# Q split low half first, two copies of each attention unit issued as DMAs, and partition changes in the planner's costs

## The chip, the cores and the metric

One NeuronCore of a Trainium2 chip runs the whole program. The metric is device time in microseconds of one execution. Engines are named as in the profile: PE (TensorE), DVE (VectorE), ACT (ScalarE), POOL (GpSimd) and SP (SyncE, which issues every DMA of this kernel).

## The reference

Attention with a learned decay bias, then two feed-forward stages, each on the output of the one before. Shapes: q, k, v are (4, 8, 576, 64), x is 2304 tokens by 512, and the hidden sizes are 2048 and 1536.

```
scores = q @ k.T / sqrt(D)                      # per batch and head, causal
cum    = cumsum(max(s, 0));  bias = min(-(cum_i - cum_j), 0)
attn   = softmax(where(causal, -1e9, scores + bias));  o = attn @ v
x  = o laid out as (B*S, H*D)
h  = x @ w_in;  x = (h - tanh(h)) @ w_out       # first stage
a  = x @ w_a;  b = x @ w_b;  out = (a * b) @ w_out2   # second stage
```

## The kernel before

Every fp32 matrix is split into two fp16 halves, a high one and a low one, and a product is made of three fp16 products: high with high, high with low, low with high. The work is cut into blocks of 256 tokens. A block j of attention has four units, one for each pair of heads; there are eight blocks and 32 units. Blocks 0 to 3 hold the first two tiles of 128 queries of a batch, blocks 4 to 7 the last two and the 64 rows that are left over (a "merged" unit, with pool "rest" and longer keys). The first feed-forward stage of a block runs as soon as its attention is done and shares the engines with the attention of later blocks. The second one comes last.

The path of one unit, with the names that the text uses. `g_load` issues the loads of q, k and v, `g_scale` works out powers of two for scaling, `u_split` writes the halves of q and k into the tile qk, and writes three rows of ones, scaled, into qB at partitions 64 to 66. `u_turn` transposes qk with one DMA into qkT: the first 64 partitions of qkT are then the first halves that were stored, the last 64 the second ones. The score product is made of two matmuls (`u_qk`): one of qkT with qkT over 128 partitions, one of qB with kB over 67 partitions, of which the last three carry the bias (kB rows 64 to 66 come by a small DMA, `u_load`).

The high half of q is stored first, so that qkT holds q high in partitions 0 to 63 and q low in 64 to 127, beside k high and k low in the same places. `u_turn` (lines 1079 to 1081) then makes three copies of 64 partitions: k high into kB, q low into qB, and q high over q low in qkT (the doubled half). With these, the 128-row matmul gives q high with k high and with k low, and the 67-row one gives q low with k high and the bias. Each copy may run on ACT, DVE or POOL (`copy_scaled`, an `either` of three engines).

What sets the order. The program records each operation in a `Plan`, and `run` then simulates five queues (PE, DVE, ACT, POOL, SP): at each moment it takes from the ready operations of a free engine the one with the earliest due time, chooses the engine of an `either` by the costs in `cost`, and emits it. The due times are written out, one for each operation, in the string ORDER (four characters each), which `follow` reads only if their number is that of the recorded operations. On the chip each engine runs its instructions in the emitted order and waits for semaphores. Tiles come from pools with fixed numbers of buffers (qkT 3 and kB 3 in blocks 0 to 3, 2 each in the merged ones; qB 2; qk 2, and 1 in the merged ones). POOL operations that read, and some of DVE, take turns at a port that they share (`shares`, `lock`). All DMAs, transposes too, go through SP's one queue in emitted order.

Since all operations are emitted by one wrapper, most of the profile's rows carry line 648; tiles tell them apart.

Of the kernel before, what the change touches and what calls it, by code (L numbers as in the profile page):

```python
# [14 lines left out]
F32 = mybir.dt.float32  # L15
# [23 lines left out]
    "IbhkIAOqH/9fIACMIADLH/8mIAVxIAX4IAavIAZiIAIWIAZ7IAazIAmEIARbIAYGIAMIIAm2IAjXIAcWIAYQIATCIASAH/1qH/9TIAI2IAJoIAAmIAAZH//a"  # L39
    "H/+fIAUcIAXaIAWaIAXHIAXcIAZiIATlIAWBIATOIAWXIAXXIAQIIAYgIAU3IAQbIAHjIAYLIAVzIAUcIAVoIAWNIAX3IAdiIAeEIAdUIAgYIAQ/IAhOIAfd"  # L40
    "IAU8IAhJIAirIAjVIAizIAj3IAmPIAgTIAnDIA06IAPGIAfaIAftIAQ5IAg/IAhcIAjpIAj5IAkMIAp8IAk0IAojIA0iIAr3IA/sIAc+IAj+IAfdIAg0IAd2"
    "IAh0IAYLIAnGIAnzIAseIAhCIAtqIAyXIAnAIAxXIAwZIA1uIA3EIA1rIA6lIBE5IA7xIA6aIAdYIAy3IA2CIAxgIA2zIAuvIA2eIA6zIA68IA9rIA66IA+6"
    "IA9HIBCAIBJYIAaxIAUpIAdBIAXnIAZuIAXpIAeSIAe3IAd1H//qIAb1IAhDIAekIAmCIAfnIAgsIAj7IAk8IAmfIAh5IAizIBC/IAhXIAjmIAmhIAlmIAnv"
    "IAqiIAqKIAqtIAziIA0RIA6+IA71IA70IA/fIA/OIA/pIBAvIA3jIBEkIBD8IBASIBAUIBDFIA6MIA+wIA/SIA7XIA4uIA8pIBFdIBDaIBCEIBDEIBBNIBDG"
    "IBHlIBQJIBSaIAfNIAluIAuMIAq6IAtjIA81IAmuIA9eIA8HIA/sIBCRIBAyIBGAIBChIBGtIBHoIBPeIBICIBOPIBVBIBMSIBWrIBIXIBCmIBKHIBLwIBGz"
    "IBL9IBLBIBLQIBIwIBQvIBL6IBToIBSxIBQTIBV6IBcrIEStIENAICz+IC52ICoQIClqICtCIClFICUkICNxICQwIAmXIAx6IA2hIA6BIAh8IAheIAm9IAz+"
    "IA3gIBERIBGfIBP4IBXFIBi6IBmPIBpMIBI3IBWNIBaxIBb2IBfcIBsRIBxbIB0YIBfIIBqTIBwPIBw/IBrtIB1TIB4+IB6DICAAIB9IICE7ICGLICAZICFq"
    "ICJRICMxICSNICX7ICcmICg6IBxlICD4ICQAICmiICSnIChnICitICpiICtxIC5PIDCGIDC5ICz1IDCYIDEGIDKuIDKrIDlZIDT0IDZVIBV8IBe6IBYDIBjL"
    "IBhrIBhPIBfmIBtVIBgjIBnVIBUjIBooIBZ0IBlyIBnTIBo2IBwpIBthIB06IBzlIB0fIB1IIB40IB7XIB8IIB+nICBcICC7ICFvICIQIB+SICKlIB/RICFL"
    "ICCZIBx+ICT5ICV2ICn7ICaUICOKIB9dICOXICShICHHICStICdKICa8ICT7ICflIChzICh4ICoBICW9ICu6IC3MIC2/IC3NIC+XIC7BICqxICwvICxfICvf"  # L50
# [175 lines left out]

# [114 lines left out]
class Plan:  # L341
# [140 lines left out]
    def run(self, switch=None):  # L482
# [1348 lines left out]
```

## Time and profile before

| | |
|---|---|
| time, median of 3 runs | 974.56 us (972.02 to 976.58) |
| profiled execution | 972.53 us |
| its span, first to last instruction | 970.8 us |
| PE busy | 907.7 us (94%), 7974 matmuls |
| DVE, ACT, POOL busy | 794.6, 557.3, 211.0 us |
| granted TensorE clock, mean | 0.995 |
| DMA | 109.23 MB, mean 113 GB/s |

The share of an engine is an average over stages that differ. The attention with the first feed-forward stage takes the span up to some 575 us, the second feed-forward stage the rest. A row of the window view gives the busy time of each engine in one stretch, and what is missing to the length of the stretch is idle time.

### The profile page before, as it was taken

To read this page: it belongs to the slowest core of one execution; us is meant where nothing else is said; L and a number is where in the kernel's file an instruction comes from. 1 tells how busy PE (TensorE), PEld (TensorE's weight loads), DVE (VectorE), ACT (ScalarE), POOL (GpSimd) and SP (SyncE) were. 2 spreads that over 40 slices of the span, in tenths; PEclk is the share of its full clock that TensorE was granted. 3 is DMA by queue.
4 is the path that set the end of the run, shared out by engine and by line. 5 is a ranking of instruction groups with operands and counts; after the bars stand their busy time and mean duration, and the time that the engine had idled before them with its cause. 6 is when DMAs were issued, how large, how long until landed. Compare 5 with 4: busy or idle time off the path is not lost.

```text
span 970.8 us, 21004 instructions
## 1 busy us (share of the span) xinstructions
PE 907.7 (94%) x7974; PEld 686.0 (71%) x7974; DVE 794.6 (82%) x2038; ACT 557.3 (57%) x1112; POOL 211.0 (22%) x322
## 2 busy tenths in 40 slices
PE   1699899999999989999999999999999999999998
PEld 0477678877777777777888877544477777777865
DVE  8899999789999899898899899997277478545635
ACT  6899889767887688786898653331131232112311
POOL 2132222213443454452112200110021011000000
PEclk9999999999999999999999999999999999999999
DMA  8999764348997687989755410200020011001001
GB/s 205 224 313 278 162 131 105 73 115 168 188 189 161 133 168 155 180 184 159 264 210 182 149 45 12 76 1 1 1 88 1 1 45 44 1 1 44 1 1 44
DMA packets 255973, 109.23 MB, mean 113 GB/s; under 512 B 216897, under 2 KB 239665, under 8 KB 255873
## 3 DMA queue, kind: packets, MB, share of 16 engines
q1 hardware_dynamic: 255872, 107.90, 46.6%
q8 instruction: 62, 1.02, 0.4%
q14 instruction: 39, 0.31, 0.1%
HBM read 60.53 MB, written 11.17 MB: 74 GB/s over the span
## 4 chain that ended last, share of the span: by engine, by line
PE 54%; DVE 17%; DMA 7%; ACT 5%; issue 3%; SPq 2%; POOL 1%; POOLq 0%; DVEq 0%; ACTq 0%
PE h L648 19%; PE qk L648 14%; PE acc L648 13%; PE pv L648 8%; DVE qk L648 3%; DVE w L648 2%; SPq L648 2%; DMA qkT<-qk 2%; DVE a L648 2%; DVE ghl L648 2%; DMA raw<-in_v_dram 1%; DMA xf<-in_moe_w_out_dram 1%; DVE h L648 1%; DMA aT<-a 1%; ACT xf L648 1%
## 5 line engine op out<-in xcount | busy, mean ns | idle before, releaser
L648 PEld LDWEIGHTS <-w 128*128 128x128 f16 x5160 | 497.9, 98 | 123.1 <-issue 16.1
L648 PE MATMUL h<-xhl,w 128*128 128x256 f16 (+1 forms) x2256 | 291.2, 279 | 3.1 <-DVE g L648 1.9
L648 PE MATMUL acc<-ghl,w 128*128 128x256 f16 x1536 | 190.5, 272 | 1.8 <-DVE ghl L648 1.7
L648 PE MATMUL h<-xf,w 128*128 128x256 f16 (+1 forms) x560 | 88.2, 307 | 2.5 <-ACT xf L648 1.8
L648 PEld LDWEIGHTS <-ghl 128*128 128x128 f16 x432 | 42.3, 98 | 45.4
L648 ACT ACTIVATE sq<-h 128x512 f32<-128x512 f32 x36 | 21.5, 597 | 83.5 <-PE h L648 82.8
L648 DVE CUSTOM_DVE_ANT_0 qk<-qk,caus,cs 128x384 f32<-128x384 f32 (+3 forms) x120 | 64.2, 555 | 2.3 <-PE qk L648 1.8
L648 PE MATMUL acc<-w,ghl 128*128 128x512 f16 x252 | 60.9, 379 | 0.0
L648 PE MATMUL qk<-qkT 128*128 128x128 f16 (+4 forms) x168 | 45.5, 316 | 14.2 <-DVE qkT L648 9.4
L648 ACT ACTIVATE th<-h,xc 128x512 f32<-128x512 f32 x64 | 43.6, 681 | 12.3 <-PE h L648 10.1
L648 ACT ACTIVATE w<-w 128x1024 f32<-128x1024 f32 (+1 forms) x42 | 48.2, 1156 | 2.5 <-DVE w L648 1.7
L648 PEld LDWEIGHTS <-v 128*64 128x64 f16 x1440 | 37.5, 112 | 12.2 <-issue 9.6
L648 ACT ACTIVATE sq<-raw 128x576 bf16<-128x576 f32 (+2 forms) x57 | 38.6, 678 | 12.8 <-DMA raw<-in_k_dram 5.2
L648 PE MATMUL qk<-kB,qB 67*128 67x128 f16 (+4 forms) x168 | 45.2, 314 | 0.0
L648 PE MATMUL qk<-w,ghl 128*128 128x512 f16 x180 | 43.7, 379 | 0.0
L648 PEld LDWEIGHTS <-sq 128*128 128x128 f16 (+1 forms) x234 | 22.9, 98 | 23.3 <-issue 0.3
L648 ACT ACTIVATE w<-xf 128x512 f16<-128x512 f32 x30 | 18.7, 630 | 34.8 <-DVE xf L648 26.9
L648 PEld LDWEIGHTS <-qkT 128*128 128x128 f16 (+1 forms) x176 | 16.4, 103 | 31.4 <-DVE qkT L648 15.6
L648 DVE SCALAR_TENSOR_TENSOR ghl<-h,xsg,ghl 128x512 f16<-128x512 f32 x48 | 35.6, 743 | 3.6 <-ACT ghl L648 3.5
L648 DVE SCALAR_TENSOR_TENSOR h<-h,xc,th 128x512 f32<-128x512 f32 x48 | 36.0, 749 | 2.6 <-ACT th L648 2.6
L648 DVE TENSOR_TENSOR g<-g,h 128x512 f32<-128x512 f32 x36 | 24.5, 684 | 16.1 <-PE h L648 14.3
L648 ACT ACTIVATE qk<-qk,nm 128x512 f32<-128x512 f32 (+1 forms) x56 | 31.7, 566 | 10.1 <-DVE nm L648 9.7
(277 smaller groups left out, 1764.8 us busy)
## 6 DMA issues: line engine op xcount, KB each, us to landing
w<-in_moe_w_out_dram SPq DMA_DIRECT2D x8, 1024.0 KB
w<-in_moe_w_in_dram SPq DMA_DIRECT2D x6, 1024.0 KB
x_d<-x2hl SPq DMA_DIRECT2D x18, 256.0 KB
w<-in_moe_w_a_dram SPq DMA_DIRECT2D x4, 1024.0 KB
xhl<-x_d SPq DMA_DIRECT2D x4, 1024.0 KB
out_dram<-x2f SPq DMA_DIRECT2D x16, 256.0 KB
ws<-in_moe_w_out_dram SPq DMA_DIRECT2D x3, 1024.0 KB
xf<-in_moe_w_b_dram SPq DMA_DIRECT2D x3, 1024.0 KB
```

Of the source, the lines that this page charges most:

```text
L648: return getattr(getattr(plan.nc, name), what)(*[real(a) for a in args], **{k: real(a) for k, a in kw.items()})
```

## The change

1. `split` takes the place of the high half as a parameter. For q it is 1: the low half is stored first, for k and v nothing changes. After the transpose qkT holds q low beside k high and q high beside k low, so that the 128-row matmul gives the two cross products without a further copy. The third copy of `u_turn` is gone. qB now receives q high.
2. The two copies that stay (k high into kB, q high into qB) are DMAs from SBUF to SBUF, issued by SP, for the units of blocks 1 to 7 (`u.j` not 0). Block 0 keeps engine copies.
3. The scaled ones are written to all 128 partitions of qB, from partition 0, ahead of the copy into its first 64.
4. The tile `fac` and its three memsets are gone; the factors are constants of `tensor_scalar` instructions.
5. The planner adds a constant (MOVE, 113 ns on DVE, 129 on ACT, 95 on PE) when an instruction's start partitions differ from those of the one before it on its engine.
6. ORDER is written anew, with 4490 due times in place of 4522.

```diff
+MOVE = {"vector": 113.0, "scalar": 129.0, "tensor": 95.0}
...
+        fn.place = [fns[0].place, fns[-1].place]
...
+                    if e in MOVE:
+                        to, end = op.fn.place if type(op.fn.place) is list else [op.fn.place] * 2
+                        if at.get(e, to) != to:
+                            op.dur += MOVE[e]
+                        at[e] = end
...
+            fn.place = place(name, rd, wr)
...
+def place(eng, rd, wr):
+    if not wr or eng not in MOVE:
+        return None
+    if eng == "tensor":
+        return wr[0].p1 - wr[0].p0 == 64
+    return wr[0].p0, rd[0].p0 if rd else 0
...
-    fac = fixed.tile([P, 3], F32, name="fac")
...
-        small("tensor_tensor", out=g.inv, in0=g.inv, in1=fac, op=ALU.mult)
-        small("tensor_tensor", out=g.cs[:, 0:1], in0=g.inv[:, 0:1], in1=g.inv[:, 1:2], op=ALU.mult)
+        small("tensor_scalar", out=g.inv[:, 2:3], in0=g.inv[:, 2:3], scalar1=2.0 ** -14, scalar2=1.0, op0=ALU.mult, op1=ALU.mult)
+        small("tensor_scalar", out=g.cs[:, 0:1], in0=g.inv[:, 0:1], scalar1=g.inv[:, 1:2], scalar2=-0.125,
+              op0=ALU.mult, op1=ALU.mult)
...
-    def split(t, raw, sc):
-        copy_scaled(t[:, :, 0, :], raw, sc)
-        lo_part(t[:, :, 1, :], raw, sc, t[:, :, 0, :])
+    def split(t, raw, sc, hi=0):
+        copy_scaled(t[:, :, hi, :], raw, sc)
+        lo_part(t[:, :, 1 - hi, :], raw, sc, t[:, :, hi, :])
...
-        split(qk[:, 0:n], u.g.raw["q"][:, u.r * n:(u.r + 1) * n], u.g.sc[:, 0:1])
+        split(qk[:, 0:n], u.g.raw["q"][:, u.r * n:(u.r + 1) * n], u.g.sc[:, 0:1], 1)
...
-        copy_scaled(
-            u.qB[D:D + 3], onesh[D:D + 3, 0:n * P].rearrange("p (a c) -> p a c", c=P), u.cs[D:D + 3, 1:2])
+        copy_scaled(u.qB, onesh[:, 0:n * P].rearrange("p (a c) -> p a c", c=P), u.cs[:, 1:2])
...
-        copy_scaled(u.kB[0:D], qkT[0:D, n:], 1.0)
-        copy_scaled(u.qB[0:D], qkT[D:P, 0:n], 1.0)
-        copy_scaled(qkT[D:P, 0:n], qkT[0:D, 0:n], 1.0)
+        for o, x in ((u.kB[0:D], qkT[0:D, n:]), (u.qB[0:D], qkT[D:P, 0:n])):
+            if u.j:
+                pl.sync.dma_start(o.rearrange("p a c -> p (a c)"), x.rearrange("p a c -> p (a c)"))
+            else:
+                copy_scaled(o, x, 1.0)
...
-        nc.vector.memset(fac[:, 0:1], 1.0)
-        nc.vector.memset(fac[:, 1:2], -0.125)
-        nc.vector.memset(fac[:, 2:3], 2.0 ** -14)
```

## Rows read from the trace of the kernel before

**Rows 1.** Windows: length, us busy of PE, PEld, DVE, ACT, POOL; clock, DMA share.
```profile
0.00:50.00 50.00, 18.20 (x129) 11.93 (x129) 42.68 (x165) 36.39 (x85) 9.84 (x25) 1.00 0.93 220
50.00:200.00 150.00, 140.50 (x1154) 117.14 (x1155) 137.76 (x439) 129.29 (x276) 37.89 (x77) 0.98 0.69 172
200.00:450.00 250.00, 235.23 (x2782) 187.59 (x2780) 234.19 (x715) 199.95 (x442) 110.48 (x167) 1.00 0.85 165
...
575.00:950.00 375.00, 374.81 (x2571) 251.19 (x2570) 251.16 (x437) 93.03 (x172) 31.66 (x29) 1.00 0.06 21
```

**Rows 2.** Chain of waits, 200 to 455 us: start, us, what.
```profile
234.91 5.11 DMA qkT<-qk
...
312.59 4.09 DMA raw<-in_v_dram
...
340.95 1.31 DMA raw<-tail_d
342.26 5.84 DMA qkT<-qk
...
385.29 4.27 DMA qkT<-qk
398.34 4.57 DMA qkT<-qk
```

**Rows 3.** Timeline, 239 to 242: start, us, instruction [idle before <-releaser].
```profile
240.04 0.32 DVE L648 TENSOR_SCALAR qB<-qkT 64x640 f16<-64x640 f16 x1 [0.56 <-DMA qkT<-qk]
240.40 0.45 DVE L648 TENSOR_SCALAR kB<-qkT 64x1152 f16<-64x1152 f16 x1
...
241.23 0.17 DVE L648 TENSOR_SCALAR p2a<-p2n 128x3 int32<-128x3 int32 x1
...
241.26 0.34 PE L648 MATMUL qk<-qkT 128*128 128x384 f16 x1 [0.55 <-DVE qkT L648]
...
241.31 0.81 DVE L648 SCALAR_TENSOR_TENSOR v<-raw,sc,v 128x576 f16<-128x576 f32 x1
```

**Rows 4.** Timeline of SP, 200 to 250 us, first and last of 45 rows.
```profile
199.61 0.47 SPq L648 DMA_DIRECT2D raw<-in_v_dram  x1
...
249.86 1.56 SPq L648 DMA_TRANSPOSE qkT<-qk  x1
```

**Rows 5.** Windows, the instructions of tile qkT alone: its matmuls and the three copies.
```profile
50.00:200.00 150.00, 10.78 (x48) 4.68 (x48) 3.71 (x13) 9.40 (x15) 4.92 (x8) 0.98 0.69 172
200.00:450.00 250.00, 32.64 (x112) 9.67 (x112) 11.86 (x31) 9.98 (x13) 3.73 (x4) 1.00 0.85 165
```

**Rows 6.** Timeline, 0 to 45 us.
```profile
18.78 0.29 DVE L648 TENSOR_SCALAR qkT<-qkT 64x512 f16<-64x512 f16 x1
...
19.13 0.29 PE L648 MATMUL qk<-qkT 128*128 128x128 f16 x1 [5.79 <-DVE qkT L648]
...
23.35 0.29 PE L648 MATMUL qk<-qkT 128*128 128x128 f16 x1 [2.76 <-DVE qkT L648]
```

**Rows 7.** Waits of PE from 0 to 50 us: total us, times, longest.
```profile
PE pv L648 <- ACT sq L648: 13.8, 4, 4.8
PE qk L648 <- DVE qkT L648: 8.6, 2, 5.8
```

**Rows 8.** Windows by stage, the stretch with the least PE idle time.
```profile
150.00:200.00 50.00, 49.34 (x532) 42.92 (x531) 41.47 (x146) 38.87 (x95) 9.84 (x24) 1.00 0.42 92
```

**Rows 9.** Groups by shape: line, engine, operation, count | busy us, mean ns | idle before.
```profile
L648 ACT ACTIVATE z<-z,nm 128x640 f32<-128x640 f32 x16 | 13.2, 827 | 4.2 <-DVE nm L648 3.9
...
L648 ACT ACTIVATE qB<-onesh,cs 3x640 f16<-3x640 f16 x9 | 7.4, 823 | 0.3
...
L648 DVE TENSOR_SCALAR kB<-qkT 64x1152 f16<-64x1152 f16 x13 | 6.1, 467 | 1.8 <-DMA qkT<-qk 1.7
```

**Rows 10.** Tile raw, loads as SP issues them: ns min/median/max of one issue.
```profile
L648 SPq DMA_DIRECT2D raw<-tail_d x16: 549/572/1062, 196.8 to 406.8; - x16
```

More of the change, by code (lines that the diff above doesn't have):

```diff
@@ L187 @@
[L187 to L189 removed]
+    "Ibk/IAc4IACIIAHrIAHSIAJCIARpIAUIIATrIAVSIAX2IAVlIAWrIAXbIAamIAmgIAU4IATYIAbYIAeXIAiVIAiBIAirIAhlIAg6IAFEIAGAIAH2IAG7IAJt"
+    "IAIyIAXDIAWlIAaAIAePIAZ1IAxdIAcyIAcuIAdBIAbBIAqGIBFNIAinIAnkIArjIA7lIAgJIAggIAfHIAdOIATGIAr9IAiRIApgIAp/IAzAIAtGIA1qIAqn"
@@ new lines @@
+    "IAuMIAx3IAymIAzZIA8YIA+UIA2vIA4XIA8JIAt6IAvlIAynIAtYIAv7IAxRIA0wIA0QIA3VIA2XIAwaIA2WIA9jIBAEIA+7IAu4IAhyIAjmIAT+IAjyIAow"
+    "IAkBIA26IAveIA3pIA4CIA5hIAyeIA1GIAxGIA6xIA89IA86IA+UIA+WIBABIA8iIA16IA7GIA8NIAzLIA8DIA8tIA/NIA9IIBBqIA+VIBAdIBALIA+LIBKH"
+    "IBIFIAh/IAhJIAfgIAaiIAalIAf5IAj9IAecIAmEIAZWIAiYIAvdIAs5IAtIIAoMIAqdIA2hIBPPIAyGIAwMIA7kIBHdIA2FIArRIAvCIAozIAtoIAycIA04"
+    "IA5hIA8yIA+gIA+bIA+lIA/IIBCVIBCQIBCnIBESIBE6IBFBIBDwIBAPIBJMIBAEIBBpIBBfIBBDIBB4IBHhIA7HIBIAIBH1IBHhIBNZIBEEIBJiIBX7IBWi"
@@ new lines @@
+    "IAygIAmYIAyjIA0FIA1QIA6XIAvsIA/KIA/tIBGDIBH/IBI0IBGCIBKQIBKbIBJtIBNDIBQeIBOUIBPKIBN5IBJRIBCtIBJEIBXjIBIAIBMKIBNpIBNrIBR+"
+    "IBV9IBbrIBYaIBRRIBSMIBVKIBs8IFJ5IFMoIFS3IE/BIE8mIFJLIEdHIEyXIDXbIDm8IDw4IAjuIAuIIA2BIAzfIAs0IA1+IA5TIA2UIA9xIBHpIBH5IBJo"
+    "IBNnIBH7IBaiIBiWIBVdIBY2IBklIBfwIBYkIBoUIBvfIBzpIBcKIBvuIByhIB4kIBjLIB3nIB4dIB7TIBfYIB/TICEGICK4ICEhICPIICQ7ICRBICHwICfM"
+    "ICfdIClLIB+jICMIICIGICgYICcjIC0sICxAICvKICtLICuoIDAKIDCIICvKIDBrIDFfIDIvIDNMIDO8IDQ3IDYsIBJHIBRvIBLnIBUaIBhwIBh7IBuaIByy"
@@ new lines @@
+    "IByIIBw0IBHWIBo6IBgeIBjoIBjiIB0DIB8oIB4+ICA3ICAMIB2CICChIB8+IB9LICD4ICEdICCnICI0IB9+ICRFICFsICExICJzICMQICPsICXYICeTICar"
+    "ICflICdFICYhICRvICUZICY7ICXbIChSICp7ICnTICwmICnGICodICnsICjMICqNICvdICxDICvWIC45IDFTIDAWIC2QIC0kICwkIC3UIDHTIC6aIDLhIDNA"
+    "IDCfIDHcIDX/IDPbIDSHIDN/IDMPIDN7IDiqIDf1IDfIID5JIDkiIDvYIBGDIBJSIBSEIBWlIBIUIBVSIBXuIBVwIBqaIA9OIBJYIBVyIBVqIBLKIBXFIBYF"
+    "IB55IB6/IBXSIBL9IBavIBdiIBejIBgNIBibIB9QICENIBmNIBlPIBqzIBriIBzLIBpEIBq+ICDlICH6IB1xIBv6IBx9IB1XIB+RIB05IB+9ICMgICNxIB1t"
@@ new lines @@
+    "IB68IB+vICJHICXhICE2ICIBICZwICmSIB8ZIB+xICDfICF+ICPrICGkICPaICooICv9IB+2ICCfICHmICKhICMyICJHICW+IC3bIC24ICV1ICPuIChHICqD"
+    "ICuFIClrICyeIDJ+IDNDICgrIB7TICrrICxIIC+FICz3IC+1IDRoIDLbICqdICJuIC6gIC9fIDCKIC+wIC/FIDRcIDStIC0+ICvOIDJ1IDLrIDMmIDbuIDU6"
+    "IDZ+IDfPIDKsICp+IDCGIDGMIDGAIDO3IDcCIDt8IDnaIDE+IDDQIDG0IDbSIDT3IDdFIDaOID8eID2/IDQAIDM6IDOzIDTIIDPrIDe5IDfdIEFMIEKsIDpE"
+    "IDReIDeZIDilIDjkID9KIEIvIESnIEVXIDV2IDKtIDrkIDm2IDqZIFapID93IEv1IE2qIQUfIFSaIbt5ILQKILIWIGZCIGJZIMxQIH/AIFxrIF02IBEEIBLu"
@@ new lines @@
+    "IA5fIBHHIA7aIA4UIBUyIBWYIBEdIBYRIBS5IBLhIBYjIBVFIBYbIBY1IBg8IBgMIBjTIBezIBhYIBhfIBwyIBX8IBjuIBYaIBhHIBllIBh7IBzCIByvIB1u"
+    "ICESICGRICD4ICHYICJuICOmICQlICTeICUjICTLICT6ICQDIB4MICC+ICIvIB3LIB/NICCtICKlICO4ICRpICYdICQjICTjICbcIB+yICnGIBxiIBkAIBnE"
+    "IBiKIBpxIBhEIB5iICEcICI3ICJ+ICRUICXFICODICYEICZQICf4ICiQICh3ICofIChsICkiICpDICLoICZkICawICJlICdJICdvICh2ICioICkaICnLICk7"
+    "ICnkICn9ICkBIC8jICAGIB3+IB1JIBvtIB5vICMBICCEICLyICKyICFsICg0ICmVICKLIClIICpcICqLICoRICvsICw9ICleICxbICkMICIlICmqICqZICMZ"
@@ new lines @@
+    "ICpVICuPICg8ICs7ICu1ICyGIC2NIC4nIC24IC1cIDFmICKhICEeICUNICCDICLLICdpICUeIClGICo1ICG2ICuXICxZICBHICxrICwVIC3zIC/tIC52IDBw"
+    "IC83IC7cIDA+ICWLIC16IC6eICecIC5wIC83IDAbIDDKIDIvIDBEIDDDIC93IDBiIDRqIDRxIDWpIDUbIDZYIDgFIDd4IDeZIDeeIDaAIDc4IDiGIDf8IDhP"
+    "IDknIDlmIDoLIDl1IDrzIbmnIDp6IDm+IDpXIDrSIDhWIDiAIDj1IDlGID2bID3dID5JID7eIDuOIDuWIDtkIDosIDqBIDuCIDqZIDyBID+zIEEDID97IEDg"
+    "IDxcIDy5IDzLIEApIEEYIEQEIEFaIENcIER2IEJBIEOmIEZPID/LIEL+IEGBIENrIELPIEOiIENaIEQ7IElnIEWFIEnUIEfSIEJnIENrIEPmIERNIEMdIEPy"
@@ new lines @@
+    "IEUdIEaXIEsOIEtLIEojIEniIETiIEUZIEaQIEe3IEduIEhaIEr2IEwLIErvIE1xIEucIE5OIEgaIEjPIElHIEj0IEkdIElrIEtXIEuhIE9JIE6qIE+UIFLw"
+    "IEwVIEx8IEzjIE09IE0kIE74IE9/IFGFIFDxIFFZIFNiIFHPIFSzIFXAIFcsIGAmIGsKIGGcIG03IHPSIbmuIG6oIKGMIKq3IPHTIG6hIG5XII3JIPB5IC95"
+    "IDBfICgMICxmICvrIC4SIDGCIC9mIDFiIC5VICobIDPtIDUDIDMpIDSwIDUSIDVVIEQ5IDZ/IDWqIDl4IDulIDVUIDWgIDajIDSeIDXHIDZOIDhZIDlWIDc6"
+    "IDt/IDx1ID0EIDnEIDvVID7pIDrwID3ZID50ID6UID6QID59ID7bIDp0IDywID0kIDzLID2LID6EID5yID3nID/6ID+KID4lID+OIEAzIEJUIEYRIDuxIDYU"
@@ L190 @@
+    "IbDGIbFVIa5wIa8VIbHWIbI7IbKRIbCaIbDXIbZlIbenIbBcIbF2IbR/IbVtIbKqIbWkIbjqIbnyIbmNIbpQIbFdIbIiIbPmIbXkIbM2IbYbIbNDIbZYIbsh"
+    "IbuTIbMAIbiIIbqVIbsDIbt2IbsSIbvEIb1/IcTbIbpIIbsNIbvdIbw4IbyFIb1uIbyAIb2qIcENIcFxIbrvIbtDIbzDIb2hIb1CIb3xIcBpIcEeIcFfIcIH"
+    "IcEiIcHAIcJnIcLQIcM3IcIjIcLCIcdeIcihIcGdIcJhIcOHIcRGIcL/IcR9IcYKIccUIcb/IcetIcJAIcL/IcLkIcSyIcOBIcToIcQrIcUkIcauIcdiIcT1"
+    "IcbVIcgLIchxIcivIcc0Icj6IcqSIcszIcnjIcvUIcyOIcz5IcqrIcsVIcvtIcxYIcymIctMIcu2IcwE"
 )
@@ L492, in run @@
         port = 0.0
+        at = {}
         def offer(op):
```

267 lines of the change are left out of this document (116 added, 151 removed).

## The prediction

> **What bounds the kernel now.** I read the page's busy times first: PE is busy 907.7 of the span's 970.8 us, so at most 63.1 us are to be had while its matmuls stay as they are, and the change leaves every matmul in place. The windows by stage say where those lie [rows 1]: 31.8 us in the first 50, 9.5 from 50 to 200 (blocks 1 to 3 of attention beside the first feed-forward stage), 14.8 from 200 to 450 (the merged blocks), 0.2 in the 375 us from 575 on; the 6.8 that are left lie between 450 and 575 and at the very end. The second feed-forward stage is out of reach: PE has no gap there. What the change can give is a part of the 56 us of gaps before 450; what it can take is new gaps.
>
> Next, who makes those gaps. From 50 to 450 DVE is busy 92 and 94% of the time, ACT 86 and 80%, POOL 25 and 44% [rows 1]. PE needs what DVE and ACT make, and DVE has hardly a free slot, so I read a gap on PE there as DVE being late. The chain of waits for the merged blocks adds a second cause: its longest pieces are transposes of qk on their way to landing, four of 4.27 to 5.84 us [rows 2], and behind such a landing the three copies run one after another before PE may start, from 240.04 to 241.26, 1.22 us [rows 3].
>
> Last SP's queue. Between 200 and 250 us its 45 rows of DMA issue sum to 41.5 of 50 us [rows 4], 83%. It is no free engine.
>
> **The change part by part.** The sum is made against the profiled execution, 972.53 us (the span and 1.7 us around it). The median of the runs shown, 974.56, is 2.0 us above; I carry the sum over to it at the end.
>
> *Three copies of a unit leave DVE, ACT and POOL.* On these engines, tile qkT's instructions are these copies and nothing else [rows 5]. For the 28 units of blocks 1 to 7 all three go, for the four of block 0 only the third.
>
> Start, 0 to 50. The first score matmul waits for the third copy: it starts at 18.78 and PE at 19.13 [rows 6], so without it PE could start some 0.3 us earlier. For the second unit PE idles 2.76 us up to the same copy [rows 6]. But of PE's waits here the larger part, 13.8 us against 8.6, is for ACT's sums of squares [rows 7], and DVE is at 85% [rows 1], so what PE gains early it partly waits for later. Bounds: -0.3 (the first wait only) and -3.1 (both). I take -1.0, nearer the lower end, since DVE's own saving is four copies of 0.29 us at most.
>
> Blocks 1 to 3, 50 to 200. DVE loses 3.71 us of 137.76, ACT 9.40 of 129.29, POOL 4.92 of 37.89 [rows 1, 5]. The stage can shorten by what its fullest engine loses, or more if ACT was the late one. Bounds: 0, and -7.5, since in the best stretch of this stage PE idles 0.66 us in 50 [rows 8], which over 150 would leave 2.0 of the 9.5. I take -3.0, just under DVE's own share. The DMAs that come instead I put at nothing here: PE has other blocks' matmuls to run meanwhile; without that cover they cost what is worked out next.
>
> Merged blocks, 200 to 450. DVE loses 11.86 us, ACT 9.98, POOL 3.73 [rows 5]. DVE loses changes of partition too: the copy of 240.04 reads from partition 64, and the next starts 0.04 us after its end, while between instructions with the same partitions the next starts before the other has ended (241.31 against 241.40) [rows 3]; a change costs some 0.12 us. Of the 31 DVE copies 13 are those of kB [rows 9], which involve no partition 64; the other 18 make about 2.2 us. DVE gets 14.1 us lighter where PE idles 14.8. Bounds: 0 and -14.1. I take half, -7.0, a choice: DVE is the fullest, but the chain shows that transposes and loads hold a part of the gaps, which a lighter DVE does not close.
>
> *The DMAs that come instead.* Two for a unit, 80 KB into qB and 144 KB into kB, both waiting for the transpose. No row shows a copy from SBUF to SBUF. The nearest is the load of the tails, 96 KB: 0.57 us of SP for the issue [rows 10] and 1.31 us from there to the landing; the slowest load in the chain took 4.09 [rows 2]. Two issues and one landing are 2.45 us (at most 5.2) in place of the 1.22 of DVE's copies: +1.2 us for a unit. Bounds: 0, where the copies ran on ACT (823 ns for 640 columns [rows 9], so three of them over 2.4 us), and +4.0. It counts on the path where the chain goes through qkT's transposes, 4 of the 16 units [rows 2]: +4.9. If it were all 16, +20. The stage comes to -7.0 + 4.9 = -2.1.
>
> The Trainium skill, "DMA: Bandwidth & Descriptors", section "Anatomy of one DMA — SWDGE (gpsimd) path", gives a DMA a fixed cost of some 2.0 us whatever its size, plus its bytes over 436 GB/s, which I estimate by its figures at 2.3 us for the larger copy, against the row's 1.31; by it the four passes would cost +8.9 and this stage would lose 2 us. The tails' load lies below that fixed cost and the chain's other load above it [rows 2], so I keep the row. The same page, section "Issuing engines are not separate DMA queues", holds the time to issue a DMA to be small beside the DMA itself; this trace disagrees, 0.57 us against 1.31 [rows 2, 10].
>
> *SP's queue.* 32 more issues of 0.57 us are 18 us in 250, which takes SP from 83 to 90%. Behind each stand, in order, the transposes of attention weights (aT), the next unit's loads and the next qkT. At the mean that fits, so it is no term; where it stops fitting is the first rival. The bytes are 3.7 MB on the 41 MB of this stage (165 GB/s over 250 us), where the DMA engines' share is 0.85 [rows 1]: 0.93 at most.
>
> *Edits at nothing.* The ones over 128 partitions instead of 3: on ACT 640 columns take 827 ns on 128 partitions and 823 on 3 [rows 9]. Two small instructions of a group's scaling are replaced by two of no more columns, and the three memsets go. The order of q's halves changes no instruction's size. If the ones did cost more on 128 partitions, DVE and ACT would show it, as their slack hides nothing.
>
> *The new order.* All due times are rewritten, with the planner's costs. No row tells its worth; it can close or open gaps, and the bounds above hold for it too.
>
> Sum: -1.0 - 3.0 - 2.1 = -6.1 us, 966.4 for the profiled execution, 968.5 on the scale of the median. I say 968.5.
>
> **The rivals.**
> 1. *SP becomes the bound of the merged blocks.* Its 42 free us in 250 are used up when each of the 32 new DMAs holds the queue for 1.3 us, issue and wait for the transpose's landing together. Landings take 4 to 6 us [rows 2]; an order that puts the copies right behind the transpose makes SP wait them out, with aT's transposes and the loads behind it. For it: SP at 83%, and an issue of a tail load that took 1.06 us [rows 10]. Against: the planner offers a copy to SP only when its model has the transpose landed, and emits other issues meanwhile. Price: if all 16 units lose the 1.2 us, +20, against -1.0, -3.0 and half of the -7.0: +12.5, 987 us on the median's scale; if half of them lose it, +2.5, 977.
> 2. *Nothing moves.* The gaps belong to latency (transposes, loads) rather than to DVE's load, and the lighter engines wait more. For it: ACT and POOL have room already, and PE still idles. Against: DVE at 94%. Price: only the -1.0 of the start, and 3 us of either sign from the order: 971 to 977.
> 3. *The gaps close further.* DVE's relief counts in full and the DMA copies are hidden: -3.0 - 7.5 - 14.1 = -24.6, 950 us; half of that is 962. For it: the stretch of rows 8. Against: the transposes in the chain, which stay.
> 4. *The change doesn't do what it says*: if the number of due times did not match the operations, the order would be ignored. It has 32 fewer due times, and 32 units have one copy less, so 1 in 100, without a price.
>
> **How the numbers follow.** A measurement of this kernel tells some 0.5%, 4.9 us, from no change (the three runs shown spread over 4.6 us). I give the forecast 0.42, the further closing 0.13, no movement 0.26, SP as the bound 0.18. The forecast's own range is 962 to 972; one part in eight of it lies above 969.7. Faster: 0.42 x 0.88 + 0.13 + 0.02 of rival 2 = 0.52. Slower, above 979.4: 0.13 of rival 1 and 0.03 of rival 2 with a bad order, 0.16. Same: 0.32. The range from 955 to 981 leaves out the better half of rival 3 and the worse half of rival 1, some 0.16.
>
> **What would show it.** In the trace after: DVE's busy time lower by 16 to 21 us between 0 and 450 and ACT's by some 20; PE's busy time the same within 2 us, with gaps of 6 or 7 us from 50 to 200 and 12 or 13 from 200 to 450; the first score matmul 0.3 us earlier; SP near 90% from 200 to 250, its new issues at 0.4 to 0.7 us each; 2 to 3 us from a transpose's landing to the unit's first matmul instead of 1.2. I am wrong if PE's gaps after 200 grow, if SP's rows show waits of over a microsecond for qkT with aT behind them, or if PE's busy time itself changes.

## The result, and the profile after

The changed kernel takes 978.96 us (median of 9 runs, 978.14 to 981.66) against 974.56 for the kernel before in the same comparison (9 runs). The ratio is 1.0051, with a 95% interval of 1.0032 to 1.0069: slower by half a per cent, where I had said 968.5. That lies inside the range that I gave (955 to 981), but on the other side of the kernel before. Its profiled execution took 978.82 us with a span of 977.0, 6.2 more than before.

PE's busy sum grew from 907.7 to 912.6 us with the same 7974 matmuls, and its gaps from 63.1 to 64.4. The stages answer to [rows 1]; the columns are those of that group:

```profile
0.00:50.00 50.00, 18.09 (x131) 12.12 (x132) 42.96 (x169) 36.78 (x86) 9.23 (x24) 0.98 0.99 234
50.00:200.00 150.00, 144.34 (x1182) 120.91 (x1181) 135.11 (x442) 118.08 (x256) 41.19 (x74) 0.96 0.83 183
200.00:450.00 250.00, 228.07 (x2679) 181.10 (x2678) 219.63 (x676) 177.98 (x403) 88.16 (x134) 0.97 0.88 172
...
575.00:950.00 375.00, 375.00 (x2583) 252.33 (x2581) 262.14 (x456) 99.15 (x181) 28.90 (x26) 1.00 0.06 22
```

PE's idle time fell from 9.5 to 5.7 us between 50 and 200 (in part because its matmuls ran slower there, at a mean clock of 0.96 against 0.98) and rose from 14.8 to 21.9 between 200 and 450, though DVE, ACT and POOL all got lighter there. So the merged blocks lost. The next lines tell how PE's waits of 200 to 450 divide after the change (total us, times, longest). Of the tiles, sq holds squares whose sums ACT takes for scaling, zs exponentials by ACT, nm the rows' minima by DVE, and ghl the halves of a feed-forward tile:

```profile
PE qk L655 <- DMA kB<-qkT: 9.8, 7, 2.0
PE pv L655 <- ACT sq L655: 4.8, 3, 2.0
...
PE qk L655 <- ACT zs L655: 1.5, 1, 1.5
...
PE acc L655 <- DVE ghl L655: 0.7, 2, 0.4
...
PE qk L655 <- DVE nm L655: 0.2, 1, 0.2
```

The first line is the price that one sees. One such wait in the timeline from 236 to 241 (start, us, instruction, idle before it), which answers to [rows 3]:

```profile
236.28 0.47 SPq L655 DMA_DIRECT2D qB<-qkT  x1
...
236.80 0.59 SPq L655 DMA_DIRECT2D kB<-qkT  x1
...
237.90 0.33 PE L655 MATMUL qk<-qkT 128*128 128x384 f16 x1
...
237.99 1.88 SPq L655 DMA_TRANSPOSE qkT<-qk  x1
...
240.25 0.32 PE L655 MATMUL qk<-kB,qB 67*128 67x384 f16 x1 [2.03 <-DMA kB<-qkT]
...
240.63 0.38 PE L655 MATMUL qk<-kB,qB 67*128 67x512 f16 x1
```

The first of the two score matmuls no longer needs a copy and runs at 237.90. The second stands at the head of PE's queue for 2.03 us until kB has landed, and starts 2.9 us after the end of its issue. The next transpose is issued only after both copies.

Two rows measure the merged stage. The first is that of the 16 transposes aTm, one for a unit (the attention weights of the left-over rows), with their first and last start. The kernel before, then the changed one (ns min/median/max, first and last start):

```profile
L648 SPq DMA_TRANSPOSE aTm<-am x16: 1281/1373/2057, 229.7 to 457.0; - x16
```
```profile
L655 SPq DMA_TRANSPOSE aTm<-am x16: 1321/1544/2132, 232.9 to 465.0; - x16
```

From first to last that is 227.3 us before and 232.1 after: 4.8 us more. I call it the aTm stretch below. The second is that of the transposes qkT, with which the same 16 units begin:

```profile
L648 SPq DMA_TRANSPOSE qkT<-qk x16: 1296/1598/2428, 206.6 to 435.4; - x16
```
```profile
L655 SPq DMA_TRANSPOSE qkT<-qk x16: 1514/1940/3050, 202.7 to 440.7; - x16
```

The merged blocks began 3.9 us earlier than before and took 9.2 us longer from their first qkT to their last (238.0 against 228.8). So the stages ahead of them gained, and the merged blocks lost more than the aTm stretch tells: in the new order the first aTm comes 30.2 us behind the first qkT, before it was 23.1. Between runs of one order the aTm stretch compares like with like.

### The profile page after: what moved, and what is told of

Read it like the earlier page. It is cut to its first block, busy times and chain, and to the rows that moved or that the text cites. A ratio compares the mean times of both kernels' runs of the same rounds, so it can differ in the third digit from the quotient of the medians.

```text
span 977.0 us, 20949 instructions
## 1 busy us (share of the span) xinstructions
PE 912.6 (93%) x7974; PEld 690.5 (71%) x7974; DVE 789.2 (81%) x2030; ACT 531.0 (54%) x1067; POOL 188.0 (19%) x282
## 4 chain that ended last, share of the span: by engine, by line
PE 47%; DVE 9%; DMA 2%; SPq 2%; issue 1%; ACT 1%; POOL 0%; DVEq 0%; ACTq 0%
PE h L655 16%; PE qk L655 13%; PE acc L655 11%; PE pv L655 7%; DVE w L655 3%; SPq L655 2%; DVE ghl L655 2%; DMA w<-in_moe_w_a_dram 1%; DVE xf L655 1%; DVE h L655 1%; DMA xf<-in_moe_w_b_dram 1%; DVE qk L655 1%; DVE a L655 0%; DVE g L655 0%; DMA qB<-qkT 0%
## 5 line engine op out<-in xcount | busy, mean ns | idle before, releaser
L655 PE MATMUL h<-xhl,w 128*128 128x256 f16 (+1 forms) x2256 | 296.8, 281 | 0.2 <-DVE xhl L655 0.2
L655 PE MATMUL acc<-ghl,w 128*128 128x256 f16 x1536 | 193.6, 274 | 2.0 <-DVE ghl L655 1.8
L655 DVE CUSTOM_DVE_ANT_0 qk<-qk,caus,cs 128x128 f32<-128x128 f32 (+3 forms) x120 | 64.7, 556 | 7.4 <-PE qk L655 5.9
L655 PEld LDWEIGHTS <-v 128*64 128x64 f16 x1440 | 37.4, 112 | 10.1 <-issue 8.4
L655 PEld LDWEIGHTS <-sq 128*128 128x128 f16 (+1 forms) x234 | 22.9, 98 | 23.1
L655 DVE SCALAR_TENSOR_TENSOR a<-qk,sm,a 128x512 f16<-128x512 f32 (+1 forms) x56 | 35.3, 631 | 1.9 <-ACT a L655 1.8
L655 PE MATMUL pv<-aT,v 128*64 128x128 f16 x960 | 34.7, 224 | 2.0 <-DMA aT<-a 1.9
L655 DVE TENSOR_TENSOR xf<-w 128x512 f32<-128x512 f16 x53 | 36.4, 720 | 0.0
```

What stands on the lines that cost most here:

```text
L655: return getattr(getattr(plan.nc, name), what)(*[real(a) for a in args], **{k: real(a) for k, a in kw.items()})
```

## The experiments

### The planner's own reruns

The first four kernels left the planner in charge. e1: all copies on engines. e2: DMAs for blocks 1 to 3 alone. e3: for the merged blocks alone.

```diff
-            if u.j:                        # after
+            if False:                      # e1
+            if u.j and not u.merged:       # e2
+            if u.merged:                   # e3
```

e4 also takes before's due times, without those of the third copies, and MOVE is empty.

> The changed kernel and its due times, but the two copies of every unit stay on ACT, DVE or POOL (no SBUF-to-SBUF DMA); the third copy stays out. Landing theory (the second score matmul of a merged unit stands at the head of PE's queue and waits for copies that land some 3 us after their issue): PE's waits for kB and qB by DMA, 10.7 us in the changed kernel, are gone, PE's gaps from 200 to 450 us fall from 21.9 to 15 or less, granted clock in that stretch back from 0.97 to 1.00; 967 to 972 us. Order theory (the rewritten due times and the planner's partition costs are worse by themselves): 975 to 980 us, gaps near 22 us with other releasers. Queue theory (SP's queue is overfull): also 967 to 972, but the rows of SP from 200 to 250 must fall from 44.4 to some 41 us.

> The changed kernel with DMA copies in blocks 1 to 3 only; the merged units (blocks 4 to 7) copy on engines. Landing theory: the first part of the gain stays (gaps from 50 to 200 us about 5.7 as in the changed kernel, 9.5 before), the loss of the merged units goes: 965 to 970 us. Order theory: 975 to 980 us. Queue theory: 966 to 971 us, as SP is full only from 200 us on.

> The changed kernel with DMA copies in the merged units only; blocks 1 to 3 copy on engines. Landing theory: all of the loss stays and the gain of blocks 1 to 3 goes: PE waits for kB and qB by DMA near 10 us again, 979 to 984 us. Order theory: as the changed kernel, 977 to 981. Queue theory: as the landing theory.

> The changed kernel with all copies on engines, no partition costs in the planner, and the due times of the kernel before, less the 32 of the third copy: what is left of the change is q low half first, without the third copy. Landing theory: the lighter engines are a small gain, 966 to 973 us. Order theory: the same, but then the first kernel of this job (same instructions, new due times) must be slower than this one by 5 us or more.

Measured against before: e1 989.4 us, 1.0143 (1.0125 to 1.0162); e2 984.7, 1.0091 (1.0075 to 1.0107); e3 989.7, 1.0138 (1.0116 to 1.0159); e4 993.4, 1.0190 (1.0168 to 1.0212). All are slower than the changed kernel, whatever was undone, and above every range that the expectations gave. Due times are fitted to one set of operations and durations; with another set, the simulated queues take another order everywhere. These runs measure that order, not the edit.

So for the rest I recorded the emitted sequence (operation and engine) of the kernel before and of the changed one, and replayed it. Where an operation is dropped or replaced, nothing else moves on any engine (the traces of e8 and of the changed kernel have the same instructions in the same order on PE, DVE and POOL). The code from here on is shortened:

```diff
-        pl.follow(ORDER)
-        pl.run(switch)
+        pl.replay(switch)      # emits EMIT, the recorded (operation, engine) list
```

### The third copy alone, in before's order (e5)

```diff
+        split(qk[:, 0:n], ..., 1)                            # q low half first
-        copy_scaled(qkT[D:P, 0:n], qkT[0:D, 0:n], 1.0)       # dropped from EMIT
```

> The kernel before, with every instruction emitted in exactly the order and on the engine that it had there; q is split low half first and the third copy of each unit (16 in all) is left out of that order. No DMA is added and the planner decides nothing. The copies' theory (a copy that leaves is worth its engine time where DVE was late for TensorE): 0.995 of before, about 970 us, TensorE's busy sum in 200 to 450 up from 235 to 238. The landing theory says nothing of this run. The order theory (the engines follow a fixed order, so a hole in it is not filled, and its worth can only be had by a new order): within 0.2% of before. A result over 1.005 would say that leaving work out of a fixed order costs by itself.

968.07 us, 0.9933 (0.9910 to 0.9956): the copies' theory holds, 6.5 us (0.0067 of 974.5) for 32 copies, one for each unit (not the 16 of the expectation; 16 were on DVE, 12 on ACT, 4 on POOL). The order theory, for which a hole in a fixed order is worth nothing, falls. PE's busy sum in 200 to 450 rose to 238, as said, and its idle time fell from 14.8 to 11.6:

```profile
200.00:450.00 250.00, 238.42 (x2879) 192.02 (x2878) 234.61 (x721) 199.74 (x445) 108.73 (x167) 1.00 0.85 167
```

Nearly the same operations under the planner were e4, at 993.4 (it also has the ones over 128 partitions and the constant factors): 2.6% apart, for the most part by order and choice of engine.

### DMAs in before's order (e6, e11)

```diff
+            if u.j:                        # e6; e11: u.j and not u.merged
+                pl.sync.dma_start(o, x)
+            else:
                 copy_scaled(o, x, 1.0)
```

> The run e5 with one difference: the other two copies of the units of blocks 1 to 16 are DMAs on SP, at the places that the copies had in the order. The landing theory (the second score matmul stands at the head of TensorE's queue until the copies have landed, 1.9 to 2.9 us after the last issue, 4 to 8 us in all, and the clock falls in the holes): e5 plus 5 to 12 us, with a wait of PE's score matmul for the DMA of kB of 7 us or more. The SP theory (two issues of 0.55 us per unit on a queue that is 83% busy push loads and stores back): e5 plus 5 us or more too, but with PE's idle time ended by raw loads or by transposes, not by kB. The forecast of mine: e5 plus 4.9 less 6. The order theory: e5 within 2 us, since the changed kernel's loss would come from its new due times alone.

> The run e5 with the DMAs in blocks 1 to 3 alone (12 units, 24 DMAs), at the places of the copies in before's order; the merged units keep their two engine copies. By the forecast's term for these blocks: e5 less 0 to 3 us, 965 to 968. By the landing theory, as the due times of before give the landing no room: e5 plus 4 us or more, since e6 lost 52 us with 28 such units, and TensorE's busy sum in 50 to 200 fell from 142.0 to 136.5.

e6: 1020.1 us, 1.0457 (1.0425 to 1.0489), 51 us above e5. e11: 976.6, 1.0014 (0.9999 to 1.0029), 7.9 above e5. PE's wait in e6 from 200 to 450, and in e11 from 50 to 200:

```profile
PE qk L675 <- DMA kB<-qkT: 25.9, 9, 5.5
```
```profile
PE qk L675 <- DMA kB<-qkT: 6.4, 4, 2.4
```

In an order that was made for engine copies the sign was as the landing theory said, and e6's size four times its upper end. My own term for blocks 1 to 3, a gain of up to 3 us, did not come in this order. In e6, PE's waits for kB and qB are 41.0 us over the whole span, against 10.7 in the changed kernel. So the new due times do hide most of the landing.

### The changed kernel's own order: copies back on engines (e7, e10, e13)

```diff
+            if u.merged:                   # e7; e10: u.merged or u.j
+                pl.vector.tensor_scalar_mul(o, x, 1.0)
                                            # e13: the qB copy by ACT, kB by DVE
```

> The changed kernel in exactly its own order and on its own engines, but the two copies of the merged units are on DVE again, at the places that their DMAs had; blocks 1 to 3 keep the DMAs. The landing theory: the wait for kB (9.8 us) goes, DVE takes 24 copies of about 0.3 to 0.6 us, and the sum is 4 to 8 us below the changed kernel, about 972. The SP theory: the same sign, with SP's busy share in 200 to 400 back at 83%. The order theory: within 2 us of the changed kernel, 979, or slower where DVE is late.

> The run e7 with the 24 copies of blocks 1 to 3 on DVE as well, so no copy is a DMA. If the DMAs of blocks 1 to 3 take work from a late DVE, as I had forecast (3 us), this is 2 to 6 us slower than e7, 972 to 975, with TensorE's busy sum in 50 to 200 down from 141.4. If the landing costs there what it costs in the merged units, it is faster than e7 by 1 us or more. If nothing is late there by DVE, within 1 us.

> The run e7 with the qB copy of a merged unit on ACT (64x640, 0.45 to 0.8 us by the neighbours) and the kB copy on DVE as there. DVE is busy 240 of 250 us in 200 to 450, ACT 185: if DVE is late for TensorE there, its 16 copies less give 1 to 4 us, 965 to 968. If the copies' latency counts, ACT's longer copy and its queue cost 0 to 4 us, 970 to 974.

e7: 969.48 us, 0.9944 (0.9924 to 0.9964), 10.4 us below the changed kernel by the ratios. e10: 974.87, 1.0005 (0.9990 to 1.0020). e13: 967.44, 0.9932 (0.9909 to 0.9955).

So in the changed kernel's order the 32 DMAs of the merged units (not the 24 of the expectation) cost 10.4 us (e7 against after) and those of blocks 1 to 3 gain 5.9 (e7 against e10). What the SP theory said of e7's queue did not come: the rows of SP's timeline from 200 to 400 sum to 180.0 us, 90% and not 83%, against 184.8 in the changed kernel. The stage of e7 from 200 to 450, and its aTm stretch (220.8 us):

```profile
200.00:450.00 250.00, 232.72 (x2834) 187.70 (x2832) 239.90 (x743) 185.20 (x420) 92.99 (x140) 1.00 0.86 164
```
```profile
L682 SPq DMA_TRANSPOSE aTm<-am x16: 1262/1589/3059, 229.9 to 450.7; - x16
```

DVE is 96% busy there, and PE idles 17.3 us against the 21.9 of the changed kernel, where DVE is 88% busy: the fuller engine is the faster kernel. (e7's profiled execution, 964.94, is the fastest of its ten; the ratios, not this row, carry the sizes.) e13 takes 16 copies off DVE again and is not measurably faster than e7 (1.2 us by the ratios, each sure to some 2). The rows of e7 and e10 from 50 to 200 show the other sign:

```profile
50.00:200.00 150.00, 141.36 (x1203) 118.70 (x1202) 135.42 (x443) 119.34 (x263) 41.53 (x74) 1.00 0.82 182
```
```profile
50.00:200.00 150.00, 139.87 (x1133) 115.65 (x1134) 138.31 (x453) 115.32 (x249) 40.94 (x73) 0.97 0.76 169
```

With the copies on DVE (e10, the second row) PE idles 10.1 us against 8.6 with DMAs and gets through 70 matmuls fewer, a part of that at a lower clock. That DVE was late there, as I had forecast, fits; no row shows it alone. e5, e7 and e13 beat both kernels, and they can't be told apart.

### Is it the wait, or the queue? (e8, e9)

e8 issues the DMAs from ACT's queue (`pl.scalar.dma_start`). e9 puts up to 2.7 us of feed-forward matmuls (the expectation's expert matmuls), which stood right behind it, ahead of the unit's first waiting score matmul; nothing else moves.

> The changed kernel in exactly its own order and on its own engines, with one difference: the two DMAs of a unit are issued from ACT's queue and not from SP's. The landing theory: within 2 us of the changed kernel (979), since the landing is the same; the wait for kB stays between 6 and 10 us. The SP theory: 4 us or more below it, SP's busy sums in 200 to 400 back at about 42 of 50, the wait for kB under 4 us. If ACT's own queue holds the DMAs behind its work, slower than 981.

> The changed kernel with all its DMAs, in its own order but for one thing: ahead of the first score matmul of a merged unit that reads the two copies, 0.7 to 2.7 us of expert matmuls (median 2.6, 14 of 16 units; two units have none that may go first) that stood right behind it on TensorE now run first. The landing theory (the loss is the score matmul's place at the head of TensorE's queue while the copies land): the wait for kB falls from 9.8 to under 4 us and the time from 979 by 4 to 8 us, to 971 to 975, though DVE, ACT and SP do what they did in the changed kernel. The SP theory and the order theory: no gain, 978 to 984.

e8: 978.55 us, 1.0037 (1.0020 to 1.0053), not to be told from the changed kernel. Its waits from 200 to 450:

```profile
PE qk L682 <- DMA kB<-qkT: 3.7, 2, 3.0
PE qk L682 <- DMA qB<-qkT: 3.2, 4, 1.6
```

The waits fell from 10.7 to 6.9 us and SP's rows from 200 to 400 (summed over four stretches of 50 us) from 184.8 to 171.6, as the SP theory had asked (some 42 of 50, the wait for kB under 4 us); the time that it then forecast, 4 us less, did not come. ACT took the 32 issues, 0.48 and 0.51 us each (median), and their waits, so the run does not decide, but it speaks against SP's queue as the whole cause.

e9: 984.37 us, 1.0102 (1.0081 to 1.0123), slower, where the landing theory wanted 971 to 975 and the other two no gain (978 to 984):

```profile
PE pv L682 <- ACT sq L682: 6.2, 7, 2.7
PE qk L682 <- ACT zs L682: 3.6, 5, 1.3
PE acc L682 <- DVE ghl L682: 3.2, 5, 1.0
PE qk L682 <- DMA kB<-qkT: 3.1, 2, 2.4
PE qk L682 <- DVE nm L682: 2.7, 4, 1.4
```

The wait for kB fell from 9.8 to 3.1 us as meant, and the waits for sq, zs, ghl and nm rose from 7.2 to 15.7. The hole moved down the unit's chain. A wait in the table names where lateness shows, not what makes it.

### The DMAs as load alone (e12, e14, e17, e18) and one of two (e15), and POOL's queue (e16)

These take e7, where DVE makes the copies, and add 32 DMAs into rows of kB and qB that nobody reads.

```diff
                 pl.vector.tensor_scalar_mul(o, x, 1.0)
+                pl.sync.dma_start(idle, x[0:61])          # e12
+                pl.sync.dma_start(idle, x[0:48])          # e14
+                pl.sync.dma_start(idle, onesh[0:48])      # e17: a constant tile
+                pl.gpsimd.dma_start(idle, onesh[0:48])    # e18: POOL's queue
```

In e17 and e18 each moves 640 elements of a partition.

e15 leaves kB a DMA and puts qB's copy on ACT. e16 is the changed kernel with its DMAs issued by POOL.

> The run e7 (969.5) with the 32 DMAs of the merged units put back as load alone: each is issued on SP where the changed kernel issues it, moves rows of the same tile and of the same length (61 partitions of 64) into rows that nobody reads, and the score matmul waits for DVE's copy only. If the changed kernel loses because a unit's scores come a landing later, this is within 2 us of e7, 968 to 972. If it loses because of what two more issues and transfers do to SP's queue and to the other DMAs, this loses what the changed kernel loses against e7, 975 to 980.

1081.0 us, 1.1104 (1.1074 to 1.1134), far outside both. SP's timeline from 250 to 262:

```profile
250.80 0.62 SPq L682 DMA_DIRECT2D qB<-qkT  x1
251.46 0.57 SPq L682 DMA_DIRECT2D kB<-qkT  x1
252.13 0.81 SPq L682 DMA_DIRECT2D kB<-part_d  x1
253.04 8.19 SPq L682 DMA_TRANSPOSE qkT<-qk  x1
```

The transpose behind the two took 8.19 us, against a median of 1.6 for e7's. The control was worse than what it stood for.

> The run e12 with its idle DMAs on 48 partitions in place of 61, all else the same (e12 gave 1081.0, with raw loads and transposes on SP 5 to 8 us long behind the idle DMAs; 61 rows don't divide evenly over 16 DMA engines, 48 do, and so do the 64 of the changed kernel). If the 61 rows were what made e12 slow, SP's transposes are back at about 2 us. Then: if the changed kernel loses by the later arrival of the two tiles, 968 to 973, near e7 (969.5); if by the load of the 32 DMAs, 975 to 980. If it stays above 1000, the load of such DMAs on SP's queue is far dearer than in the changed kernel and the control says nothing of it.

> The changed kernel in its own order with the kB copy of a merged unit by DMA as there, and the qB copy on ACT as in e13 (967.4). Arrival: the score matmul needs both tiles, so one DMA late is nearly as bad as two, 974 to 979, with a wait for kB of 6 us or more. Load: half of the loss is back, 971 to 975, with a wait for kB under 5 us.

> The changed kernel in its own order, with the two DMAs of a unit issued from POOL's queue; POOL is busy 88 of 250 us in 200 to 450, SP 182 of 200. If SP's queue pays for the DMAs (their issue, and SP standing still at one until the transpose before it has landed), the time falls to 968 to 974. If the later arrival of the tiles is what costs, as e15's wait for kB of 7.6 us says, 976 to 982 with that wait still over 6 us. If POOL's issue of a DMA is long or stands behind POOL's own work, over 984.

> The run e14 (983.9) with one difference: the idle DMAs read a constant tile (48 partitions, 640 elements) in place of the transposed one, so SP has nothing to wait for at them; issue and place stay, the kB one moves 640 elements in place of 1152. If the wait at the head of SP's queue is what e14 paid, near e7, 968 to 974. If the two issues of 0.55 us and the transfer on a busy queue are, 979 to 985.

> The run e17 (982.5) with the 32 idle DMAs issued from POOL's queue, 0.565 us each by e16, in place of SP's; the same tiles and bytes move, and again nobody waits for them. If SP's issue time is what e17 and e14 paid (32 by 0.59 us on a queue busy 175 of 200 us in e7), the time is back near e7, 968 to 973, with SP's busy sum in 200 to 400 near 175. If the transfers themselves disturb the other DMAs, 978 to 985. If POOL's 18 us of issue count, in between, with PE waiting for POOL's tiles.

e14: 983.86 us, 1.0089 (1.0062 to 1.0116), above both of its ranges. e15: 974.86, 0.9995 (0.9976 to 1.0013). e16: 992.93, 1.0185 (1.0161 to 1.0210). e17: 982.48, 1.0088 (1.0071 to 1.0104). e18: 975.24, 0.9996 (0.9978 to 1.0014).

The aTm stretches of e14, e17 and e18, one after the other:

```profile
L682 SPq DMA_TRANSPOSE aTm<-am x16: 1281/1447/2993, 234.2 to 471.9; - x16
```
```profile
L682 SPq DMA_TRANSPOSE aTm<-am x16: 1252/1718/3027, 233.6 to 467.3; - x16
```
```profile
L682 SPq DMA_TRANSPOSE aTm<-am x16: 1255/1812/3297, 233.9 to 461.0; - x16
```

237.7, 233.7 and 227.1 us, against e7's 220.8. In e17 nobody waits for the DMAs (but for one inferred wait of POOL, 3.3 us) and they wait for no transpose, yet they cost 14.0 us (1.0088 less 0.9944). With the same DMAs issued by POOL (e18), 9.0 of the 14.0 are back, and the intervals of e17 and e18 don't meet. e18 changes two things, though: SP is spared the issues, and the transfers leave the DMA queue in which SP's transposes and loads stand (q1 in the profile) for another (q0). If the transfers held up what stands behind them, transposes would land later after their issue in e17. They don't. Counted by the semaphore updates in the traces (16 for each DMA, 4 for the small load of kB; the counts close), the medians from the start of an issue to its landing, from 200 to 450 us, are 4.55, 4.56 and 4.45 us for qkT and 4.72, 4.58 and 4.69 for aT in e7, e17 and e18. So SP's issue time is the larger part of this load: 32 issues of some 0.59 us are 19 us on the queue through which each unit's qkT, aT and aTm must also pass. The other 5.0 I can't divide: transfers, POOL's 32 issues of 0.55 us, or waits of POOL, whose DMAs also take their turn behind DVE by the program's rule for the shared port. e18's 975.24 lies between its ranges.

e15, with one DMA in place of two, stands 6.1 us above e13, and PE waits again:

```profile
PE qk L682 <- DMA kB<-qkT: 7.6, 7, 1.7
```

Its 974.86 lies in both theories' ranges; the wait sides with the arrival. e16 failed as its last case had it; its DMAs stood behind POOL's own work and, by the same rule, behind DVE's, so it says little of SP:

```profile
PE qk L682 <- DMA kB<-qkT: 12.5, 6, 5.9
PE qk L682 <- DMA qB<-qkT: 6.9, 3, 3.5
```

## Why the prediction was wrong

The sum, rebuilt from runs of fixed order, each step a difference of two ratios times 974.5 us (each ratio is sure to some 0.2%, so each step to 2 or 3 us): the third copy out, -6.5 (before to e5); the new order, with the other copies all on DVE, +7.0 (e5 to e10, and e10 also has the ones over 128 partitions and the constant factors, which e5 lacks); DMAs in blocks 1 to 3, -5.9 (e10 to e7); DMAs in the merged units, +10.4 (e7 to after). Together +5.0.

*Three copies of a unit leave the engines.* The start: the first matmul on qkT ran at 17.19 in place of 19.13, 1.9 us earlier and not 0.3, but PE's busy time up to 50 is the same, 18.09 against 18.20, so nothing of the -1.0 shows by then. Blocks 1 to 3: said -3.0; the merged blocks began 3.9 us earlier, and the runs of fixed order give -5.9 for the DMAs of blocks 1 to 3. The merged blocks: said -7.0 for a lighter DVE. In the order of before, the third copy alone did close 3.2 us of PE's gaps there (e5). In the changed kernel DVE's sum fell by 14.6 us in 200 to 450 [rows 1], near the 14.1 worked out, and PE's gaps grew by 7.1. In that order DVE, however full, was not what the stage waited for last: e7 runs with DVE at 96% and is faster, and e13's relief of it gave nothing measurable.

*The DMAs that come instead* is the step that failed: +4.9 said, +10.4 measured for the merged units, and the 10.4 is net of what DVE gets back. One part of it is the landing. I took that of a tail load for 1.31 us [rows 2], and misread the row: a piece of the chain ends where the next piece begins, here with the transpose's issue at 342.26. By the semaphore updates in the trace of before that load landed at 343.35, 2.4 us after its issue began, and the tail loads of this stage took 2.3 to 4.4 us, median 2.7. The changed kernel's copies took about as long, a median of 2.67 us for kB and 2.45 for qB. With 2.7 the same working gives one issue and 2.7 less 1.22, 2.05 us a unit in place of 1.2, or +8.2 in place of +4.9. So the load was the right neighbour, and its issue is a fifth of it, not near a half. The Trainium skill, "DMA: Bandwidth & Descriptors", section "Anatomy of one DMA — SWDGE (gpsimd) path", which I set aside for that row, is nearer with its estimate of 2.3, though its path is that of POOL's DMAs and these are SP's. But e9 shows that hiding the wait at PE's head does not bring the time back.

*SP's queue* is the other part, and got no term at all, "at the mean that fits". SP's rows from 200 to 250 sum to 44.4 us, 89%, as forecast; the three stretches of 50 us behind it to 47.2, 46.1 and 47.1. That share alone shows nothing, as e7 has 90% without these DMAs. What shows the cost is the load put back: e17 gives 14.0 us for the issues and transfers alone, 9.0 of them gone when POOL issues. My first rival had the place right. That its price for half of the units, 977 us, was near the measured 979 is luck: it is made of the misread 1.2 us a unit and has nothing for the order. Its reason, SP waiting out a landing, is not needed: e17's DMAs wait for no landing and cost what e14's cost, which do. The Trainium skill, "DMA: Bandwidth & Descriptors", section "Issuing engines are not separate DMA queues", holds the issue to be usually small beside the DMA. Here it was 0.53 to 0.59 us (median) of 2.45 to 2.67, and e17 and e18 show that on a full queue even that counts.

*The new order*, "no row tells its worth", was put at nothing and stands at +7.0 in the rebuilt sum (part of it may be the copies that e10 puts on DVE, or the two small edits). It bought room for the landing: e6 shows what the DMAs cost without it.

*PE's busy time the same within 2 us* failed too: +4.9, with as many matmuls. It is the granted clock, told in the last section: with the same 7974 matmuls PE's busy sum was 901.5 us at a mean clock of 0.998 (e7), 907.7 at 0.995 (before), 912.6 at 0.986 (the changed kernel) and 925.1 at 0.972 (e6). Of the signs of being wrong that I had named, two came: PE's gaps after 200 grew, and its busy time changed.

What stays open: how the 10.4 us of the merged units' DMAs divide between SP's queue (up to 14.0 by e17), the arrival (e15's wait), and what DVE's relief gives back. e8 and e16 moved the issue, but onto engines that had work of their own; e8 took 13 us off SP's rows and shortened the waits, and gained nothing that can be measured.

## What to carry to other kernels

Price a DMA that replaces an engine's copy by its issue on the queue that issues it, at that queue's load in this stage, as well as by its landing; here a queue at 83 to 90% that also carries the stage's transposes paid 9 to 14 us for 19 us of issues. Read a landing from the DMA's own updates, or from who waits for it, and not from a piece of the critical chain, which ends where the next piece begins. A busy engine is not the bound until a run with less work on it is faster. And where a list scheduler sets the order, freeze the emitted order to test an edit: nearly the same operations stood 2.6% apart under two orders, more than any edit here gained.

## What the runs showed of the hardware

In the changed kernel the granted clock fell around 300 us, where PE had idled (windows of 5 us: PE's busy us, clock, DMA share, GB/s):

```profile
295.00:300.00 5.00, 4.61 (x83) 1.00 0.67 155
300.00:305.00 5.00, 2.53 (x18) 0.89 0.99 187
305.00:310.00 5.00, 5.00 (x32) 0.77 0.54 110
310.00:315.00 5.00, 5.00 (x49) 1.00 0.91 176
```

PE was busy for 2.53 of 5 us, after a wait of 1.92 for kB at 301.52 and one of 0.95 for sq; part of the next 5 us then ran at the lower level, 1.2 in place of 2.4 GHz. From the timeline there:

```profile
301.52 0.32 PE L655 MATMUL qk<-kB,qB 67*128 67x384 f16 x1 [1.92 <-DMA kB<-qkT]
...
305.82 0.63 PE L655 MATMUL qk<-kB,qB 67*128 67x512 f16 x1
```

The same matmul took 0.38 us at 240.63. So a gap can cost twice, once as idle time and once as slower matmuls after it: of the 6.2 us of span lost, 4.9 are PE busy time. By the trace's clock records the changed kernel ran 27 us at the lower level, half of them before 200 us, the kernel before 7 (the last us apart). e7, e13 and e5 show a clock of 1.00 over 200 to 450, the changed kernel 0.97.

A DMA on 61 partitions held up what stood behind it: between 200 and 450 us the longest aT transpose took 9.6 us in e12, 3.5 in e7 without such DMAs, and 3.4 in e14 with them on 48 partitions. Why was not tried. The traces show one difference: a DMA on 61 partitions brought 2 semaphore updates, one on 48 or 64 brought 16.
